# Strided sparse attention and a multiplicative FFN on one core: weight fold and first FFN tile laid between the attention phases of the first two batches

## The chip, the cores and the metric

The kernel runs on one NeuronCore of a Trainium2 chip. The metric is the device time of one execution in microseconds. Five engines take part: TensorE (PE in the profile; its weight loads are PEld) multiplies and transposes, VectorE (DVE), ScalarE (ACT) and GpSimd (POOL) copy, cast and do elementwise work, and SyncE (SP) issues the loads. Outputs are issued from ScalarE's queue.

## The reference

For 8 batches of 8 heads, with 576 positions and a head size of 64, masked attention is computed; heads 0 to 3 see the last 32 positions, heads 4 to 7 the earlier positions with the same remainder modulo 32. The heads are joined to 4608 tokens of 512 numbers, and a feed-forward stage follows that multiplies two projections.

```python
scores = scale * np.matmul(q, k.transpose(0, 1, 3, 2))
mask_local = (rel >= 0) & (rel < stride)                 # stride = 32
mask_strided = (rel >= 0) & (pos[None, :] % stride == pos[:, None] % stride)
attn = softmax(np.where(mask, scores, -1e9))
x = np.matmul(attn, v).transpose(0, 2, 1, 3).reshape(4608, 512)
out = ((x @ w1) * (x @ w2)) @ w3 @ w_out                  # w1, w2: 512x1024; w3: 1024x1024; w_out: 1024x512
```

## The kernel before

**The fold.** There is no nonlinearity between w3 and w_out, so the kernel multiplies them once into w34 (1024 x 512) and each token needs one product less. `fold_tr(jc)` (L353) transposes one block of 128 rows of w3 in eight transposes into one bank of PSUM, and copies the halves to w3T with VectorE and ScalarE. `fold_mm(jc)` (L362) is a sum of eight 512-wide matmuls, given in two halves of four, and one copy into w34. There are eight blocks.

**Attention.** A batch is four pairs of heads, two local and two strided. The work of a pair is a sequence of phases: `ph_T` (L208) transposes q and k; `ph_S` (L238) computes scores, exp on ScalarE and the mask on VectorE, in two groups; `ph_PV` (L259), once for each group, multiplies by v (with a column of ones for the sum) and divides on VectorE; `ph_T2` (L279) transposes the result into xT. `ph_R` (L225) transposes the last 64 positions of q and k, once for a batch. All phases of all batches form one list, `stream`; `batch_end[b]` is the place in it behind which xT holds batch b. Batch 0 has 21 phases, batch 1 has 25 (with the first transposes and scores of batch 2 among them), and each later one but the last has the same 25.

**The FFN.** A tile is 512 tokens, nine in all. `ab_halves` (L297) gives 16 units of four 512-wide matmuls: eight a and eight b, one of each for every 128 columns of w1 and w2; ScalarE copies a out of PSUM, VectorE multiplies it with b into abt. `o_halves` (L341) gives eight units of four matmuls with w34 for four output blocks, each copied by ScalarE and stored.

**Order.** The program order of all matmuls and transposes is kept (`pe`, L65). `host(units, upto, lead)` (L400) writes it: it emits the units one after the other, and after each beyond the first `lead` so many phases of the stream that it arrives at `upto` with the last unit. The order of instructions on the other engines is set when the kernel is built, with loads and casts early in the program. Buffers set further waits: psF has three banks for FFN sums (tag f), psB two for scores and attention products, psM one for transposes (tag m); loads land in nine staging buffers (stgp); cast w3 blocks have four buffers (w3n). A load is followed by a cast to fp16, by the engine named in the call: "p" GpSimd, "a" ScalarE, "v" VectorE.

**The opening.** Lines 411 to 427 give the loads: w3 block 0, w_out, w3 blocks 1 to 7, q, k and v of batch 0, w1 and w2 in four groups of 256 columns, then batch 1. Lines 429 to 446 place the fold first, with six phases of batch 0 laid between its last units, then the rest of batch 0 alone; then 12 units of FFN tile 0, four with a phase each, eight output units with a phase each, and the rest of batch 1 alone. From tile 1 on (L447), every tile's 24 units carry the 25 phases of the batch after next evenly.

Of the kernel before, what the change touches and what calls it, by code (L numbers as in the profile page):

```python
# [9 lines left out]
FP16 = mybir.dt.float16  # L10
# [9 lines left out]
def kernel(  # L20
# [11 lines left out]
    nc = tc.nc  # L32
# [4 lines left out]
    P = 128  # L37
# [3 lines left out]
    KF = DF // P  # L41
# [17 lines left out]
    psF = ctx.enter_context(tc.tile_pool(name="psF", bufs=3, space=bass.MemoryType.PSUM))  # L59
    psB = ctx.enter_context(tc.tile_pool(name="psB", bufs=2, space=bass.MemoryType.PSUM))  # L60
    psM = ctx.enter_context(tc.tile_pool(name="psM", bufs=1, space=bass.MemoryType.PSUM))
# [3 lines left out]
    def pe(ins):  # L65
        return tc.keep_in_program_order(ins)

    def copy(eng, out, in_):
        if eng == "a":
            nc.scalar.copy(out=out, in_=in_)  # L70
        elif eng == "v":
            nc.vector.tensor_copy(out=out, in_=in_)  # L72
        else:
            nc.gpsimd.tensor_copy(out=out, in_=in_)  # L74
# [47 lines left out]
    w1h = consts.tile([P, KM, DF], FP16)  # L122
    w2h = consts.tile([P, KM, DF], FP16)
    w34 = consts.tile([P, KF, DM], FP16)
# [8 lines left out]
    def load_wo(g, eng):  # L133
        src = moe_w_out.rearrange("(c p) n -> p c n", p=P)
        st = stgp.tile([P, 2, DM], FP32, tag="stg")
        nc.sync.dma_start(st, src[:, 2 * g:2 * g + 2, :])
        copy(eng, woh[:, 2 * g:2 * g + 2, :], st)

    def load_w3(jc, eng):
        st = stgp.tile([P, DF], FP32, tag="stg")  # L140
        nc.sync.dma_start(st, moe_w3[bass.ds(jc * P, P), :])
        t = ffn.tile([P, DF], FP16, tag="w3n", bufs=4)
        w3n[jc] = t
        copy(eng, t, st)

    def load_w12(g):
        cs = bass.ds(g * 256, 256)
        for wd, wh, eng in ((moe_w1, w1h, "p"), (moe_w2, w2h, "p")):
            st = stgp.tile([P, KM, 256], FP32, tag="stg")
            nc.sync.dma_start(st, wd.rearrange("(c p) n -> p c n", p=P)[:, :, cs])  # L150
            copy(eng, wh[:, :, cs], st)
# [4 lines left out]
    def load_qk(b, grp, engs="pp"):  # L156
        for nm, ten, eng in (("q", q, engs[0]), ("k", k, engs[1])):
            st = stgp.tile([P, 4, 4, D], FP32, tag="stg")
            nc.sync.dma_start(st.rearrange("p h c d -> p h (c d)"),
                              ten[b, 4 * grp:4 * grp + 4, 0:NM].rearrange("h (p c) d -> p h (c d)", c=4))  # L160
            t = qkp.tile([P, 4, 4, D], FP16, tag=f"{nm}{grp}")
            copy(eng, t, st.rearrange("p h c d -> p c h d"))
            x16[(b, nm, grp)] = t

    def load_rest(b, eng="p"):
        st = stgp.tile([P, H, D], FP32, tag="stg")
        for i, ten in enumerate((q, k)):
            nc.sync.dma_start(st[64 * i:64 * i + 64], ten[b, :, NM:S].rearrange("h p d -> p h d"))
        t = qkp.tile([P, H, D], FP16, tag="r")
        copy(eng, t, st)  # L170
        x16[(b, "r")] = t

    def load_vL(b):
        vt = v16L[b % 2]
        for hp in range(2):
            hs = slice(2 * hp, 2 * hp + 2)
            st = stgp.tile([P, 2, LT, D], FP32, tag="stg")
            for h in range(2):
                nc.sync.dma_start(st[32:P, h], v[b, 2 * hp + h].rearrange("(t p) d -> p t d", p=LQ))
            for pr in (bass.ds(32, 32), bass.ds(64, 64)):  # L180
                nc.gpsimd.tensor_copy(out=vt[pr, hs, :, 0:D], in_=st[pr])  # L181
            nc.vector.tensor_copy(out=vt[0:32, hs, 1:LT, 0:D], in_=vt[96:P, hs, 0:LT - 1, 0:D])

    def load_vS(b):
        vt = v16S[b % 2]
        for hp in range(2):
            st = stgp.tile([SQ, 2, ST, D], FP32, tag="stg")
            sf = st.rearrange("p h c d -> p h (c d)")
            sv = v[b, 4 + 2 * hp:6 + 2 * hp].rearrange("h (p c) d -> p h (c d)", c=ST)
            nc.sync.dma_start(sf[0:64], sv[0:64])  # L190
            nc.sync.dma_start(sf[64:SQ], sv[64:SQ])
            nc.gpsimd.tensor_copy(out=vt[:, 2 * hp:2 * hp + 2, :, 0:D], in_=st)
# [104 lines left out]
    def ab_halves(tch):  # L297
        tok = bass.ds(tch * NT, NT)
        res = []

        def first():
            abts[tch] = ffn.tile([P, KF, NT], FP16, tag="abt", bufs=4, name=f"abt{tch}")

        for jc in range(KF):
            st = {}

            def a(jc=jc, st=st):
                if jc == 0:
                    first()
                aps = psF.tile([P, NT], FP32, tag="f")  # L310
                for ci in range(KM):
                    pe(nc.tensor.matmul(aps, w1h[:, ci, bass.ds(jc * P, P)], xT[ci][:, tok],  # L312
                                        start=(ci == 0), stop=(ci == KM - 1)))
                asb = ffn.tile([P, NT], FP32, tag="asb")
                nc.scalar.copy(out=asb, in_=aps)  # L315
                st["asb"] = asb

            def bb(jc=jc, st=st):
                bps = psF.tile([P, NT], FP32, tag="f")
                for ci in range(KM):  # L320
                    pe(nc.tensor.matmul(bps, w2h[:, ci, bass.ds(jc * P, P)], xT[ci][:, tok],  # L321
                                        start=(ci == 0), stop=(ci == KM - 1)))
                nc.vector.tensor_mul(abts[tch][:, jc, :], bps, st["asb"])

            res += [a, bb]
        return res

    def acc_halves(lhs, rhs, done):
        st = {}

        def half(hf):
            if hf == 0:
                st["ps"] = psF.tile([P, NT], FP32, tag="f", name="ops")
            for ci in range(4 * hf, 4 * hf + 4):
                pe(nc.tensor.matmul(st["ps"], lhs(ci), rhs(ci), start=(ci == 0), stop=(ci == KF - 1)))  # L335
            if hf == 1:
                done(st["ps"])

        return [lambda: half(0), lambda: half(1)]

    def o_halves(tch):  # L341
        res = []
        for ts in range(NT // P):
            def done(ps, ts=ts):
                osb = ffn.tile([P, DM], FP32, tag="osb", bufs=3)
                nc.scalar.copy(out=osb, in_=ps)  # L346
                nc.scalar.dma_start(out_r[tch * (NT // P) + ts], osb)

            res += acc_halves(lambda ci, ts=ts: abts[tch][:, ci, bass.ds(ts * P, P)],
                              lambda ci: w34[:, ci, :], done)  # L350
        return res

    def fold_tr(jc):  # L353
        js = bass.ds(jc * P, P)
        ps = psM.tile([P, 1024], FP16, tag="m")
        for kc in range(KF):
            pe(nc.tensor.transpose(ps[:, kc * P:(kc + 1) * P], w3n[jc][:, bass.ds(kc * P, P)], id16))  # L357
        pv = ps.rearrange("x (c j) -> x c j", j=P)
        nc.vector.tensor_copy(out=w3T[0][:, :, js], in_=pv[:, 0:4, :])
        nc.scalar.copy(out=w3T[1][:, :, js], in_=pv[:, 4:8, :])  # L360

    def fold_mm(jc):  # L362
        js = bass.ds(jc * P, P)

        def done(ps):
            nc.vector.tensor_copy(out=w34[:, jc, :], in_=ps)

        return acc_halves(lambda kc: w3T[kc // 4][:, kc % 4, js], lambda kc: woh[:, kc, :], done)

# [2 lines left out]
    batch_end = {}  # L372
# [4 lines left out]
    for b in range(B):  # L377
# [4 lines left out]
        for i in range(4):  # L382
            p = 4 * b + i
# [14 lines left out]
    pos = [0]  # L398

    def host(units, upto, lead=0):  # L400
        n = len(units) - lead
        p0 = pos[0]
        for i, u in enumerate(units):
            u()
            tgt = p0 + ((upto - p0) * max(i + 1 - lead, 0)) // n
            while pos[0] < tgt:
                stream[pos[0]]()
                pos[0] += 1
# [2 lines left out]
    load_w3(0, "p")  # L411
    for g in range(4):
        load_wo(g, "p")
    for jc in range(1, KF):
        load_w3(jc, "p")
    load_qk(0, 0, "ap")
    load_rest(0, "p")
    load_vL(0)
    load_qk(0, 1, "ap")
    load_vS(0)  # L420
    for g in range(4):
        load_w12(g)
    load_qk(1, 0)
    load_rest(1)
    load_vL(1)
    load_qk(1, 1)
    load_vS(1)

    fold = []
    fold_tr(0)  # L430
    for jc in range(KF):
# [2 lines left out]
        if jc + 1 < KF:  # L434
            fold.append(lambda jc=jc: fold_tr(jc + 1))
        fold.append(h1)
    host(fold, 6, lead=17)
    host([lambda: None], batch_end[0])
    load_qk(2, 0)
    load_rest(2)  # L440
    load_vL(2)
    host(ab_halves(0), pos[0] + 4, lead=12)
    load_qk(2, 1)
    load_vS(2)
    host(o_halves(0), pos[0] + 8)
    host([lambda: None], batch_end[1])
    for tch in range(1, NTILE):  # L447
        units = ab_halves(tch) + o_halves(tch)
        if tch + 1 < B:
# [44 lines left out]
```

The softmax here doesn't subtract the row's maximum and nothing guards it: scores larger than these inputs give would overflow.

## Time and profile before

The median of three runs is 306.0 us (305.58 to 307.15); the profiled execution spans 304.4 us.

| engine | busy us | share of the span |
|---|---|---|
| TensorE | 275.4 | 90% |
| TensorE weight load | 146.7 | 48% |
| VectorE | 171.1 | 56% |
| ScalarE | 143.8 | 47% |
| GpSimd | 104.7 | 34% |

The kernel reads 38.80 MB and writes 9.44 MB. TensorE's mean granted clock is 0.954. In the chain that ended last, the matmuls of the FFN (L312, L321, L335) have 61% of the span. A row of a timeline gives start, duration, engine, line, operation, output and input, and in brackets how long the engine was idle before it and what ended that. A row of a table of stretches gives the busy time of each engine in turn with the number of its instructions, then clock, DMA share and GB/s. The clock is a share of full speed, and busy times grow when it falls.

### The profile page before, as it was taken

Reading aid. Unit: us, or ns where it says so; the run is one execution under the profiler, and the core shown is the slowest. Engines: PE = TensorE matmul, PEld = TensorE weight load, DVE = VectorE, ACT = ScalarE, POOL = GpSimd, SP = SyncE. Lnnn points to the kernel's source line nnn. Section 1 sums busy time; section 2 is a strip of 40 time slices with the busy share of each in tenths; the row PEclk is TensorE's granted clock in tenths of the full one; section 3 lists DMA queues with packets and bytes.
Section 4 is the critical chain, followed back from the end, with each engine's and each line's share of the span. In section 5 each row is a group of like instructions: output and inputs, shape, how many; then the busy total and the mean of one; then the engine's idle time right before and its main releaser. Section 6 shows DMA issues by size and latency. Waiting matters only on the chain.

```text
span 304.4 us, 6140 instructions
## 1 busy us (share of the span) xinstructions
PE 275.4 (90%) x2401; PEld 146.7 (48%) x2401; DVE 171.1 (56%) x357; ACT 143.8 (47%) x263; POOL 104.7 (34%) x120
## 2 busy tenths in 40 slices
PE   2498667999779999999999999999999999999995
PEld 1154444445554545555555555555555555444442
DVE  2043665325586795686588668856764775240330
ACT  2025573366553556545554655465555544433332
POOL 5766675750256750365366445210000000000000
PEclk9999965999857999999999999999999999999999
DMA  7999999951899954994899698021012002002003
GB/s 253 413 336 207 286 348 240 246 128 41 217 256 208 269 118 133 264 221 106 268 256 237 172 250 212 2 103 37 1 38 106 0 2 103 35 2 103 34 2 138
DMA packets 58653, 48.64 MB, mean 160 GB/s; under 512 B 29184, under 2 KB 49664, under 8 KB 58624
## 3 DMA queue, kind: packets, MB, share of 16 engines
q1 hardware_dynamic: 53440, 38.81, 50.7%
q10 hardware_dynamic: 5184, 9.44, 8.4%
q8 instruction: 19, 0.31, 0.5%
q14 instruction: 10, 0.08, 0.1%
HBM read 38.80 MB, written 9.44 MB: 158 GB/s over the span
## 4 chain that ended last, share of the span: by engine, by line
PE 78%; DVE 8%; ACT 7%; DMA 3%; issue 3%; SPq 1%; POOL 0%; ACTq 0%; DVEq 0%
PE ops L335 22%; PE bps L321 20%; PE aps L312 19%; PE ps L214 5%; PE xps L268 5%; DMA st<-in_moe_w_dram 3%; PE sps L248 3%; PE ps L284 2%; ACT pte L253 2%; DVE xqs L276 2%; PE ps L357 1%; DVE ptm_105 L255 1%; ACT xT_124 L291 1%; ACT qT L70 1%; ACT osb L346 1%
## 5 line engine op out<-in xcount | busy, mean ns | idle before, releaser
L315 ACT COPY asb<-aps 128x512 f32<-128x512 f32 x72 | 42.2, 586 | 67.2 <-PE aps L312 64.3
L74 POOL CAST t<-st 128x1024 f16<-128x1024 f32 (+1 forms) x46 | 45.1, 982 | 52.0 <-DMA st<-in_k_dram 41.6
L253 ACT ACTIVATE pte<-sps 128x576 f16<-128x576 f32 (+1 forms) x64 | 38.3, 649 | 9.1 <-PE sps L248 9.1
L321 PEld LDWEIGHTS <-w2h 128*128 128x128 f16 x288 | 26.3, 99 | 31.1 <-issue 5.5
L276 DVE TENSOR_TENSOR xqs<-xps,rcp 96x384 f16<-96x384 f32 (+1 forms) x64 | 39.6, 619 | 2.0
L312 PEld LDWEIGHTS <-w1h 128*128 128x128 f16 x288 | 25.7, 99 | 23.7 <-issue 1.9
L70 ACT COPY qT<-ps 128x512 f16<-128x512 f16 (+1 forms) x48 | 22.8, 481 | 26.3 <-PE ps L214 23.5
L346 ACT COPY osb<-ops 128x512 f32<-128x512 f32 x36 | 21.1, 586 | 29.4 <-PE ops L335 27.9
L312 PE MATMUL aps<-xT_124,w1h 128*128 128x512 f16 x72 | 27.8, 386 | 1.6 <-ACT xT_124 L291 1.5
L312 PE MATMUL aps<-xT_121,w1h 128*128 128x512 f16 x72 | 28.1, 390 | 0.0
L312 PE MATMUL aps<-xT_122,w1h 128*128 128x512 f16 x72 | 28.0, 388 | 0.0
L321 PE MATMUL bps<-xT_121,w2h 128*128 128x512 f16 x72 | 27.9, 388 | 0.0
L312 PE MATMUL aps<-xT_123,w1h 128*128 128x512 f16 x72 | 27.8, 386 | 0.0
L321 PE MATMUL bps<-xT_122,w2h 128*128 128x512 f16 x72 | 27.8, 386 | 0.0
L321 PE MATMUL bps<-xT_123,w2h 128*128 128x512 f16 x72 | 27.7, 385 | 0.0
L321 PE MATMUL bps<-xT_124,w2h 128*128 128x512 f16 x72 | 27.5, 382 | 0.0
L72 DVE COPY kT<-ps 128x512 f16<-128x512 f16 (+1 forms) x36 | 18.7, 534 | 9.8 <-ACT qT L70 9.8
L214 PE MATMUL ps<-id_79,t 128*128 128x128 f16 x256 | 20.8, 227 | 2.1 <-ACT w3T_130 L360 1.4
L214 PEld LDWEIGHTS <-t 128*128 128x128 f16 x256 | 17.6, 102 | 9.2 <-issue 3.5
L181 POOL CAST v16L_99<-st 32x768 f16<-32x768 f32 (+1 forms) x16 | 13.7, 854 | 18.5 <-PE xps L268 12.1
L274 DVE RECIPROCAL rcp<-xps 96x6 f32<-96x6 f32 (+1 forms) x64 | 12.2, 191 | 13.8 <-PE xps L268 13.5
L284 PE MATMUL ps<-id_79,xqs 72*128 72x72 f16 (+1 forms) x224 | 15.0, 210 | 3.7 <-DVE kT L72 1.6
(115 smaller groups left out, 408.8 us busy)
## 6 DMA issues: line engine op xcount, KB each, us to landing
out_dram<-osb ACTq DMA_DIRECT2D x36, 256.0 KB, 2.0
st<-in_moe_w_dram SPq DMA_DIRECT2D x16, 512.0 KB, 8.6
st<-in_q_dram SPq DMA_DIRECT2D x16, 512.0 KB, 7.1
st<-in_k_dram SPq DMA_DIRECT2D x16, 512.0 KB, 5.2
st<-in_v_dram SPq DMA_DIRECT2D x32, 144.0 KB, 4.2
st<-in_v_dram SPq DMA_DIRECT2D x16, 256.0 KB, 7.1
st<-in_moe_w_out_dram SPq DMA_DIRECT2D x4, 512.0 KB, 7.2
st<-in_q_dram SPq DMA_DIRECT2D x8, 128.0 KB, 10.3
```

The costliest lines, as they stand in the source:

```text
L70: nc.scalar.copy(out=out, in_=in_)
L72: nc.vector.tensor_copy(out=out, in_=in_)
L74: nc.gpsimd.tensor_copy(out=out, in_=in_)
L214: pe(nc.tensor.transpose(ps[:, i, c * P:(c + 1) * P], src[:, c, h0:h0 + 2].rearrange("p h d -> p (h d)"), id16))
L253: nc.scalar.activation(out=pte[0:kr], in_=sps[0:kr, :, 0:288], func=AF.Exp, bias=0.0, scale=scale)
L276: nc.vector.tensor_mul(xqs[0:w, 0:m].rearrange("p i h d -> p h i d"), xv[:, :, :, 0:D], _ap(rcp, 0, [[rp, w], [4, 2], [1, m], [0, D]]))
L284: pe(nc.tensor.transpose(ps[:, t * w:(t + 1) * w], s.xqs[t // m][0:w, t % m].rearrange("p h d -> p (h d)"), id16[0:w, 0:w]))
L312: pe(nc.tensor.matmul(aps, w1h[:, ci, bass.ds(jc * P, P)], xT[ci][:, tok], start=(ci == 0), stop=(ci == KM - 1)))
L315: nc.scalar.copy(out=asb, in_=aps)
L321: pe(nc.tensor.matmul(bps, w2h[:, ci, bass.ds(jc * P, P)], xT[ci][:, tok], start=(ci == 0), stop=(ci == KM - 1)))
L335: pe(nc.tensor.matmul(st["ps"], lhs(ci), rhs(ci), start=(ci == 0), stop=(ci == KF - 1)))
L346: nc.scalar.copy(out=osb, in_=ps)
```

## The change

The fold's units are laid across all 21 phases of batch 0, with four units ahead. FFN tile 0 is laid across batch 1: six units ahead, ten with a phase each, and eight output units across the 15 phases left. The loads are interleaved in the order in which the new program needs them: batch 0 comes between the blocks of w3, and batch 1 between the groups of w1 and w2. The fold's transposes take a bank of psF instead of the one of psM. Casts of w1 go to ScalarE, and those of batch 0's q, which were there, to GpSimd. The copies of the fold's products alternate between VectorE and ScalarE. The purpose is to give TensorE work of other kinds while a phase of attention waits for exp, mask or division. From tile 1 on the text of the kernel is as before.

```diff
-        for wd, wh, eng in ((moe_w1, w1h, "p"), (moe_w2, w2h, "p")):
+        for wd, wh, eng in ((moe_w1, w1h, "a"), (moe_w2, w2h, "p")):
...
-        ps = psM.tile([P, 1024], FP16, tag="m")
+        ps = psF.tile([P, 1024], FP16, tag="f", name="trp")
...
-            nc.vector.tensor_copy(out=w34[:, jc, :], in_=ps)
+            copy("va"[jc % 2], w34[:, jc, :], ps)
...
-    for jc in range(1, KF):
-        load_w3(jc, "p")
-    load_qk(0, 0, "ap")
-    load_rest(0, "p")
+    load_qk(0, 0)
+    load_rest(0)
+    load_w3(1, "p")
+    load_w3(2, "p")
     load_vL(0)
-    load_qk(0, 1, "ap")
+    load_w3(3, "p")
+    load_qk(0, 1)
+    load_w3(4, "p")
+    load_w3(5, "p")
     load_vS(0)
-    for g in range(4):
-        load_w12(g)
+    load_w3(6, "p")
+    load_w3(7, "p")
+    load_w12(0)
+    load_w12(1)
     load_qk(1, 0)
     load_rest(1)
+    load_w12(2)
     load_vL(1)
+    load_w12(3)
     load_qk(1, 1)
     load_vS(1)
...
-    host(fold, 6, lead=17)
-    host([lambda: None], batch_end[0])
+    host(fold, batch_end[0], lead=4)
     load_qk(2, 0)
     load_rest(2)
     load_vL(2)
-    host(ab_halves(0), pos[0] + 4, lead=12)
+    host(ab_halves(0), pos[0] + 10, lead=6)
     load_qk(2, 1)
     load_vS(2)
-    host(o_halves(0), pos[0] + 8)
-    host([lambda: None], batch_end[1])
+    host(o_halves(0), batch_end[1])
```

## The prediction

> **What bounds the kernel now.** I first read the slices of the whole span, to see where TensorE is not full.
>
> ```profile
> PE   2498667999779999999999999999999999999995
> ...
> PEclk9999965999857999999999999999999999999999
> DMA  7999999951899954994899698021012002002003
> ```
>
> A slice is 7.6 us. From slice 13 (about 99 us) to the end TensorE is full at the full clock: there only less TensorE work would help, and the change removes none. Everything to win lies in the first 13 slices, where TensorE is partly idle, its clock drops twice, and the DMA row is full until about 64 us. So I cut those 95 us at the borders of the work, which the timeline gives: second fold block (13.2), first transposes of batch 0 (27.6), the clock's first fall (40.5, the fold having ended at 37.4), first matmul of FFN tile 0 (51.3), clock back (54.6), end of that tile's outputs (78.2), first matmul of FFN tile 1 (90.7).
>
> ```profile
> 0.00:13.20 13.20, 3.35 (x13) 1.29 (x13) 1.79 (x14) 1.87 (x2) 8.58 (x20) 1.00 0.85 321
> 13.20:27.60 14.40, 14.09 (x93) 7.77 (x94) 6.27 (x12) 4.46 (x7) 8.73 (x9) 1.00 1.06 282
> 27.60:40.50 12.90, 8.08 (x96) 4.86 (x96) 6.67 (x14) 8.07 (x17) 9.04 (x9) 1.00 1.06 305
> 40.50:51.30 10.80, 7.08 (x105) 5.52 (x106) 7.66 (x17) 4.82 (x9) 6.69 (x6) 0.51 1.16 309
> 51.30:54.60 3.30, 3.30 (x13) 1.24 (x12) 0.00 (x0) 1.23 (x2) 1.73 (x3) 0.54 0.82 148
> 54.60:78.20 23.60, 22.89 (x171) 11.44 (x170) 10.67 (x22) 12.52 (x25) 9.48 (x10) 1.00 0.56 147
> 78.20:90.70 12.50, 8.40 (x128) 6.91 (x126) 8.79 (x19) 7.61 (x15) 6.09 (x7) 0.64 0.94 235
> 90.70:95.30 4.60, 4.60 (x21) 1.84 (x19) 2.60 (x6) 1.23 (x2) 3.20 (x4) 0.50 1.20 257
> ```
>
> After the stretch: its length, then busy time of TensorE, weight load, VectorE, ScalarE, GpSimd; then the clock, DMA share, GB/s. TensorE busy up to 90.7 sums to 67.2 us, so 23.5 us are idle. The worst rows are those in which attention runs with nothing between its phases: 40.5 to 51.3 and 78.2 to 90.7. There the clock also falls to half, and the FFN tile behind each pays for it: at 51.3 and at 90.7 it starts at half clock, and its matmuls run 0.63 us against 0.38 us later.
>
> Why attention alone is slow, the rows at batch 1's end show; each step waits for another engine (columns: start, duration).
>
> ```profile
> 79.92 1.19 ACT L253 ACTIVATE pte<-sps 72x576 f16<-72x576 f32 x2
> ...
> 80.60 0.86 DVE L255 TENSOR_TENSOR ptm_105<-pte,maskS 72x576 f16<-72x576 f16 x1 [2.24 <-ACT pte L253]
> ...
> 81.52 0.57 PE L268 MATMUL xps<-v16S_102,ptm_105 72*128 72x65 f16 x8 [1.03 <-DVE ptm_105 L255]
> ```
>
> The last view is when weights arrive. GpSimd casts each as it lands:
>
> ```profile
> 12.14 1.04 POOL L74 CAST t<-st 128x1024 f16<-128x1024 f32 x1 [0.24 <-DMA st<-in_moe_w_dram]
> ...
> 36.04 1.35 POOL L74 CAST w1h<-st 128x1024 f16<-128x1024 f32 x1 [0.23 <-DMA st<-in_moe_w_dram]
> ...
> 40.55 1.11 POOL L74 CAST w2h<-st 128x1024 f16<-128x1024 f32 x1 [0.46 <-DMA st<-in_moe_w_dram]
> ...
> 47.77 1.34 POOL L74 CAST w2h<-st 128x1024 f16<-128x1024 f32 x1 [1.59 <-DMA st<-in_moe_w_dram]
> ```
>
> w1/w2 are complete at 49.1, so even before, the FFN could not start much ahead of 51 with all its weights; but group 0 is there at 38.6 and group 1 at 41.7.
>
> **What the Trainium skill says.** "TensorE: Matmul & The Clock Gate", Part 1, has TensorE at half clock by default and after an idle window of about 3.4 us, and at full clock after about as long of sustained work. The trace agrees: half at 40.5 after six microseconds that were 58% busy, full again at 54.6, 3.3 us after dense work began. "PSUM — Partial Sum Buffer", Engine vs sequencer instructions, has the queues of ScalarE, VectorE and GpSimd strictly first-in first-out; no row here contradicts it, and it makes a cast on ScalarE a possible plug. "DMA: Bandwidth & Descriptors", Why small descriptors are slow, expects little from 256-byte pieces; the v loads of the local heads (L179, four issues in 6.56 us) agree: while they are issued at 21 to 27 us the rate falls from about 400 to between 89 and 216 GB/s.
>
> **The change part by part.**
>
> *Fold across batch 0.* No work is added: 8 folds of eight 512-wide matmuls at 0.216 us apart (13.8 us) and 64 transposes (8 in about 0.45, 3.6 us) stay. Before, they ran dense from 13.2 to 27.6 while attention waited for loads, then attention ran alone. Now q, k and the rest of batch 0 load ahead of w3 block 1. That block's cast stood at 12.14 behind 3.0 MB; 1.25 MB of batch 0 now go first, 3 us at about 400 GB/s or 4.5 with the small pieces. I take 16.5 for the restart of the fold (bounds 14 and 19). Remaining from there: about 16 us of fold (all but one transpose group and one half) and about 6 us of attention (a later tile of 27.8 us has 24 units of 0.86, which leaves 7.1 us for 25 phases, 0.28 each): 22 us, so 38.5 if TensorE never waits. The phases need latency: 21 phases beside 19 units, where the later tiles run 25 phases beside 24 units in 27.8 us, which shows that one unit per phase hides nearly all of it. The last w3 block comes last of the same 9.4 MB that before ended with the v cast at 34.77, so its transposes stand near 36.5, with three units and five phases left, 6 us (the last chain from scores to xT takes 4 to 5 of them at the rows above): 42.5, so the loads and not TensorE set it. I add 2 us for the copies of the fold, now queued between attention's copies (bounds 0 and 7: seven blocks, up to 1 us each). Batch 0 ends at about 44.5, against 51.3.
>
> *Fold transposes in the FFN banks.* Free of cost if a bank is free: three banks for one open sum, one transpose, one next. The single attention bank no longer alternates with the fold; before, the fold waited there 0.9 us for kT, and T (L214) 1.4 us for w3T. Gain 1 to 3 us, contained in the 44.5.
>
> *Product copies alternating, and casts.* Four copies of 0.69 us leave VectorE for 0.59 on ScalarE; q casts (two of 1.05 us) leave ScalarE for GpSimd, four w1 casts of about 1.04 come to it. Net ScalarE +4.4 us over 60 us in which it is about half to three quarters busy: hidden by TensorE's units. GpSimd falls by 2 us and is paced by loads anyway. The danger is order, not size: behind a waiting w1 cast stand the exps, on which VectorE's mask and then TensorE wait. Before, the two q casts on ScalarE stood after their loads and waited for nothing. Bounds 0 and 8 us; I take 1.
>
> *Tile 0 across batch 1.* Before: 12 units, four phases with four units, eight with eight output units, 13 phases alone. Now: 6 units, ten phases with ten units, 15 phases with eight output units. Six units take 5.2 us. Ten times 0.86 plus 0.4 for a phase (0.28 as in the later tiles, and a little of its latency) is 12.6. For the 15 phases I use what eight with eight took (68.5 to 78.2, 9.7 us) and 13 alone (12.5): about 1.0 a phase, 14.5 us. Sum 32.3. Loads of batch 1 now precede w1/w2 groups 2 and 3; group 3 was cast by 49.1, and about 1.9 MB with the slow v issue (6.8 us) go before it, so I place its casts at 56 to 57. Unit 12, the first that needs it, is due at 44.5 + 5.2 + 6 x 1.26 = 57; R(1), group 2 and the v of batch 1 come as close. I take 1 us of waiting (bounds 0 and 4). Tile 1 then starts at 44.5 + 32.3 + 1, about **78**, against 90.7.
>
> *Clock.* If units fill TensorE, the second drop goes: the 4.6 us at half clock after 90.7 save 2.3. So 306.0 - 12.7 - 2.3 = **291.0 us**.
>
> The limit below: 16.5 plus the rest of TensorE's work to that point. 67.2 less some 8 us for the halved clock (half of 7.1 at 40.5, half of 3.3 at 51.3, half of about 6 after 81.5) and less 5 done by then is 54, hence 70.5, and 306 - 20.2 - 2.3 = 283.5.
>
> **Rivals.**
> - *Filled as reckoned*, 287 to 296: 291, chance 0.55. For it: the later tiles have the same mixture at 99% busy.
> - *Loads and latency take half back*: the DMA row is full to 64 us in any order, and R(1), the v of batch 1 and group 3 each arrive late by 2 to 3 us; or the clock stays at half in 16 to 45, since waiting for w3 blocks leaves gaps. 7 us of delay and the clock saving lost give 291 + 7 + 2 = 300; chance 0.25. Against it: half-clock units are denser, and density brings the clock back.
> - *Nearly ideal*: no stall beyond the sum of work, 284 to 286: 285, chance 0.10.
> - *Plugged ScalarE, slower*: the casts of w1 groups 2 and 3 stand ahead of batch 0's last exps, which then wait for group 3 at 56. Batch 0 ends near 60, tile 0 and batch 1 take 33 after it: 93, and 306 + 2.3 = 308; chance 0.10. For it: the four casts are written ahead of all attention. Against it: so were the two q casts, which ran at 23.07 and 35.14, between copies and exps.
>
> **How the numbers follow.** Forecast 291. Low 284 covers the ideal case; high 302 covers the load case and leaves most of the plugged one out. Of the load case a little lies within 0.5% of 306, and of the plugged case a little too. Faster 0.87, same 0.04, slower 0.09.
>
> **What would show it.** Right: tile 1's first matmul near 78; no slice after the third with a clock of 6 or less; w3T copies alternating with exps up to 42; batch 0's end near 44; from then the distance of two tiles' starts near 28 us as before. Wrong: ScalarE rows at L74 that wait for in_moe_w with exps behind them (plugged); TensorE rows waiting for w1h, w2h or v16L_100 (loads); transposes at L357 waiting for the fold's copies (banks); clock at half between 16 and 60 (gaps). The forecast fails upward if two of these fall together, and downward if the first load of w3 block 1 lands by 13.

## The result and the profile after

The changed kernel takes **296.98 us** (median of 4 runs, 295.90 to 297.23), against 305.96 us of the kernel before: a ratio of 0.9693, with a 95% interval of 0.9658 to 0.9729. The profiled executions span 295.2 and 304.4 us. The forecast was 291.0, with a range of 284 to 302: right in direction and within the range, 6 us too low. In what follows a time is the median of all executions of a kernel, a ratio leaves out single slow ones, and some traces are of executions 2 to 6 us longer than that median, so moments are compared within one trace.

First the slices of the whole span.

```profile
PE   2258798999789999999999999999999999999995
...
PEclk9999999999999999999999999999999999999999
DMA  7999999999979929996999580120012002003003
```

Both falls of the clock are gone in this row. The holes in slices 5 to 7 and in slice 12 are smaller (7, 9, 8 and 8 tenths, before 6, 6, 7 and 7), though the slices are now 7.4 us long instead of 7.6. In the second and third slice TensorE does less than before. The next table cuts at the same events as the one in the prediction: waiting for the second fold block (10.4 to 18.0), that block at half clock (to 22.3), the rest of the fold and batch 0 (to 49.5, the first matmul of FFN tile 0), tile 0 and batch 1 (to 82.8, the first matmul of tile 1).

```profile
0.00:10.40 10.40, 3.35 (x13) 1.29 (x13) 1.79 (x14) 1.87 (x2) 6.49 (x18) 1.00 0.82 283
10.40:18.00 7.60, 0.00 (x0) 0.00 (x0) 0.00 (x0) 0.00 (x0) 4.79 (x5) 1.00 1.15 293
18.00:22.30 4.30, 4.26 (x17) 2.05 (x18) 1.15 (x3) 0.59 (x1) 2.70 (x4) 1.00 1.24 234
22.30:49.50 27.20, 22.61 (x276) 13.96 (x275) 16.28 (x35) 18.27 (x35) 16.13 (x16) 1.00 1.11 308
49.50:82.80 33.30, 30.36 (x308) 16.63 (x309) 19.64 (x40) 22.22 (x43) 20.57 (x22) 1.00 1.00 240
```

TensorE busy is the first number after the comma. It is zero for 7.6 us, and then 83% for 27 us: the fold did not fill batch 0 as reckoned. Tile 0 and batch 1 are at 91%. As times of the work:

| | before | forecast | after |
|---|---|---|---|
| second fold block starts | 13.2 | 16.5 | 18.0 |
| batch 0 done, tile 0 starts | 51.4 | 44.5 | 49.5 |
| tile 0's start to tile 1's start | 39.3 | 33.3 | 33.3 |
| tile 1 starts | 90.7 | 78 | 82.8 |
| from there to the end | 213.7 | 211.4 | 212.4 |

So nearly all of the 9.2 us between the two spans was won ahead of tile 1 (7.9 us), and of that 6.0 us in tile 0 and batch 1; the fold stage, which was to give 6.8 us, gave 1.9. Why TensorE stands empty here, the timelines of GpSimd and TensorE show (start, duration, engine, line, operation).

```profile
12.11 1.04 POOL L74 CAST t<-st 128x1024 f16<-128x1024 f32 x1 [0.45 <-DMA st<-in_q_dram]
14.42 1.04 POOL L74 CAST t<-st 128x1024 f16<-128x1024 f32 x1 [1.27 <-DMA st<-in_k_dram]
...
16.95 1.04 POOL L74 CAST t<-st 128x1024 f16<-128x1024 f32 x1 [0.44 <-DMA st<-in_moe_w_dram]
```

```profile
18.04 1.03 PE L357 MATMUL trp<-id_79,t 128*128 128x128 f16 x8 [8.12 <-POOL t L74]
...
22.28 1.02 PE L357 MATMUL trp<-id_79,t 128*128 128x128 f16 x8
23.14 0.61 PE L214 MATMUL ps<-id_79,t 128*128 128x128 f16 x8
```

Batch 0's q and k are cast at 15.5. Their transposes (L214) could follow at once, but in TensorE's written order four units of the fold and a third transpose group stand ahead, and all but the first of these wait for w3 block 1, cast at 18.0. After 8.1 us of idle time the eight transposes at 18.04 take 1.03 us, as those at 22.28 do, against 0.61 at 23.14: half clock, though the clock column says 1.00. TensorE had not been at full clock yet: the eight transposes at 5.30 took 1.03 us as well, and those at 5.31 and 13.24 in the kernel before. The Trainium skill, "TensorE: Matmul & The Clock Gate", has half clock in Part 1 as the state by default, until about 3.4 us of sustained work. The state is as it says; it lasted longer here, for 5.1 us of work from 18.04 to 23.14. So attention starts at 23.1, and its 21 phases then take 26.4 us.

### The profile page after: what moved, and what is told of

The parts are those of the page before. It is cut to its first block, busy times and chain, and to the rows that moved or that the text cites. A ratio compares the mean times of both kernels' runs of the same rounds, so it can differ in the third digit from the quotient of the medians.

```text
span 295.2 us, 6136 instructions
## 1 busy us (share of the span) xinstructions
PE 266.9 (90%) x2401; PEld 141.0 (48%) x2401; DVE 168.7 (57%) x353; ACT 147.1 (50%) x269; POOL 101.9 (35%) x118
## 4 chain that ended last, share of the span: by engine, by line
PE 73%; ACT 8%; DVE 7%; DMA 6%; issue 2%; SPq 2%; POOL 0%; ACTq 0%; DVEq 0%
PE ops L335 21%; PE bps L321 20%; PE aps L312 19%; PE ps L214 4%; PE xps L268 4%; DMA st<-in_moe_w_dram 3%; PE sps L248 3%; DMA out_dram<-osb 3%; ACT pte L253 3%; DVE xqs L276 2%; PE ps L284 2%; ACT xT_124 L291 2%; SPq L168 1%; ACT osb L346 1%; ACT qT L70 1%
## 5 line engine op out<-in xcount | busy, mean ns | idle before, releaser
L74 POOL CAST t<-st 128x1024 f16<-128x1024 f32 (+1 forms) x48 | 47.2, 990 | 36.4 <-DMA st<-in_k_dram 21.6
L321 PEld LDWEIGHTS <-w2h 128*128 128x128 f16 x288 | 25.7, 97 | 30.2 <-issue 4.7
L312 PEld LDWEIGHTS <-w1h 128*128 128x128 f16 x288 | 25.0, 98 | 22.3 <-ACT w1h L70 0.2
L312 PE MATMUL aps<-xT_124,w1h 128*128 128x512 f16 x72 | 27.3, 379 | 2.4 <-ACT xT_124 L291 2.2
L312 PE MATMUL aps<-xT_121,w1h 128*128 128x512 f16 x72 | 27.4, 381 | 0.1
L321 PE MATMUL bps<-xT_121,w2h 128*128 128x512 f16 x72 | 27.4, 381 | 0.0
L321 PE MATMUL bps<-xT_124,w2h 128*128 128x512 f16 x72 | 27.3, 379 | 0.0
L321 PE MATMUL bps<-xT_123,w2h 128*128 128x512 f16 x72 | 27.3, 379 | 0.0
L312 PE MATMUL aps<-xT_123,w1h 128*128 128x512 f16 x72 | 27.2, 378 | 0.0
L321 PE MATMUL bps<-xT_122,w2h 128*128 128x512 f16 x72 | 27.2, 378 | 0.0
L312 PE MATMUL aps<-xT_122,w1h 128*128 128x512 f16 x72 | 27.2, 378 | 0.0
L214 PEld LDWEIGHTS <-t 128*128 128x128 f16 x256 | 16.6, 98 | 8.4 <-issue 2.1
L214 PE MATMUL ps<-id_79,t 128*128 128x128 f16 x256 | 19.5, 219 | 1.0 <-DVE rcp L274 1.0
L181 POOL CAST v16L_99<-st 32x768 f16<-32x768 f32 (+1 forms) x16 | 13.8, 865 | 10.5 <-DMA st<-in_v_dram 7.6
L181 POOL CAST v16L_100<-st 32x768 f16<-32x768 f32 (+1 forms) x16 | 13.3, 834 | 11.6 <-PE xps L268 4.9
```

What stands on the lines that cost most here:

```text
L214: pe(nc.tensor.transpose(ps[:, i, c * P:(c + 1) * P], src[:, c, h0:h0 + 2].rearrange("p h d -> p (h d)"), id16))
```

## The experiments

Each ratio is to the kernel before on the same chip; a smaller ratio is faster.

**Which part gives what.** FFN tile 0 placed as before in the changed kernel:

```diff
-    host(ab_halves(0), pos[0] + 10, lead=6)
+    host(ab_halves(0), pos[0] + 4, lead=12)
...
-    host(o_halves(0), batch_end[1])
+    host(o_halves(0), pos[0] + 8)
+    host([lambda: None], batch_end[1])
```

> The changed kernel with FFN tile 0 placed as before (12 units ahead, four phases with four units, eight with eight, the rest alone); loads and fold as changed. If the gain comes from tile 0 laid across batch 1, as the two traces say (33.3 us from tile 0's start to tile 1's start, against 39.4, and a clock fall saved), the time is 304 to 306. If the fold and the loads brought it, 298 to 300.

302.55 us, ratio 0.986 (0.983 to 0.989). The same lines the other way round, in the kernel before and with nothing else changed:

> The kernel before with FFN tile 0 laid across batch 1 as in the change, and nothing else; loads, fold, banks and casts as before. If tile 0's place gives nearly all of it, 297 to 299 us. If it needs batch 1's earlier loads and the other edits, 301 to 304.

300.47 us, 0.980 (0.975 to 0.985). Neither reading was fully right: tile 0's place gives about 2.0% by itself, all the rest 1.4% by itself, and together they give 3.1%, nearly their sum. The part of tile 0, which seems the larger (the two intervals just meet), needs none of the other edits.

The loads of before (w3 complete, then batch 0, w1 and w2, batch 1) under the new order on TensorE:

> The changed kernel with the loads in the order of before (and batch 0's q cast on ScalarE as before): all of w3 first, then batch 0, then all of w1 and w2, then batch 1. If the order of loads is needed for the gain of the fold stage: attention again starts at about 27 with little left to lay between, batch 0 ends near 51 to 52, 299 to 302. If only the order on TensorE counts: with all of w3 early the fold runs without waiting, 296 to 298.

300.33 us, 0.979 (0.974 to 0.984), the first reading. In its trace the first attention transposes wait 3.97 us for q at 22.5, and tile 0 starts at 53.2. With the loads in the old order the rest of the change gives nothing measurable: this kernel is no faster than the one with tile 0's new place alone.

**The small edits.** The fold's transposes back in the attention bank (`psM`, tag m, in L355):

> The changed kernel with the fold's transposes back in the one bank of the attention transposes. If sharing that bank would cost, with seven transpose groups between the phases and about 1.2 us for the two copies that free the bank, each by up to 1 us: 299 to 304 us. If the FFN banks are as tight, or the waits fall into others: 297.

301.55 us, 0.983 (0.977 to 0.988), against 0.969 (0.966 to 0.973) of the changed kernel: the bank is worth about 4 us, or about 6 against the second measurement of the changed kernel below. The prediction had 1 to 3 us. Its trace shows the wait of TensorE:

```profile
24.52 0.61 PE L214 MATMUL ps<-id,t 128*128 128x128 f16 x8 [1.13 <-ACT w3T L360]
...
34.36 0.61 PE L214 MATMUL ps<-id,t 128*128 128x128 f16 x8 [1.13 <-ACT w3T L360]
```

An attention transpose waits here for ScalarE's copy of a fold block out of the one bank.

The casts of w1 back on GpSimd (`"p"` for `"a"` in L148):

> The changed kernel with the casts of w1 back on GpSimd. Theory C, ScalarE's casts stand between the exps: two w1 casts of 1.05 us ran on it at 43.3 and 46.0, in batch 0's last chain; without them batch 0 ends 1 to 2 us earlier, 295 to 296 us. Rival: they fill waits, GpSimd gets more casts and these slow VectorE's masks; 297 us or up to 1 us more.

296.93 us, 0.967 (0.962 to 0.972): no difference from 0.969. Where ScalarE casts w1 in batch 0 it delays nothing that shows in the time: in the changed kernel the copy of xT at 46.9 stands behind the cast at 46.0, but the copy after it again waits 0.63 us for TensorE. All product copies on VectorE (L366):

> The changed kernel with all eight copies of the fold's products on VectorE. Four copies of 0.69 us return to VectorE and four of 0.59 leave ScalarE. If VectorE's queue holds up masks and divisions of batch 0, 298 to 299; if ScalarE's does, 295 to 296; if neither, 297.

295.64 us, 0.9615 (0.957 to 0.966), by the number the reading in which ScalarE's queue holds up batch 0. But the changed kernel, measured once more beside other kernels, gave this:

> The changed kernel itself, to compare the two others with on one chip: 296 to 298 us.

295.87 us, 0.9625 (0.957 to 0.968). So its ratio differs by 0.7% between two comparisons, and neither of the last two edits is told from it.

**Why the fold stage gave little.** Two w3 blocks ahead of q and k:

```diff
-    load_qk(0, 0)
-    load_rest(0)
     load_w3(1, "p")
     load_w3(2, "p")
+    load_qk(0, 0)
+    load_rest(0)
```

> The changed kernel with w3 blocks 1 and 2 loaded ahead of batch 0's q and k (297.0 us otherwise). Theory A, a starved start: TensorE stands empty from 10.4 to 18.0 us because w3 block 1 comes behind q, k and the rest, and that delay is carried to the end; then the second fold transposes come at about 13 instead of 18.0, batch 0 ends 4 us earlier and the time is 292 to 294. Theory B, latency of batch 0: what ends batch 0 is the chain of its phases through ScalarE and VectorE, begun by q and k; these now land 2.5 us later, and the time is 297 to 299.

295.67 us, 0.964 (0.959 to 0.970). The transposes came at 13.5, as theory A had it, but the time did not follow: it lies between the two readings, and is not told from the changed kernel. In its trace TensorE then waited 3.8 us at 26.4 for the next block, whose cast stands on GpSimd behind the four casts of v. Then the other side, attention in front:

```diff
-    host(fold, batch_end[0], lead=4)
+    fold[0]()
+    host([lambda: None], 4)
+    host(fold[1:], batch_end[0], lead=3)
```

> The changed kernel with batch 0's first four phases (both transposes of the first two pairs, the rest and the first scores) placed ahead of the second fold transposes, loads as changed. In the changed kernel q and k are cast at 15.5, but the first attention transposes come at 23.1, behind fold units that wait for w3 block 1 until 18.0. Theory B2, TensorE's written order makes attention wait and batch 0's 21 phases then need 26 us: batch 0 ends 3 to 6 us earlier, 291 to 294 us. Theory A, the w3 blocks' lateness itself sets the end: no change, 297.

297.43 us, 0.965 (0.960 to 0.971). Its timeline of TensorE:

```profile
13.09 0.61 PE L214 MATMUL ps<-id,t 128*128 128x128 f16 x4 [3.22 <-POOL t L74]
...
44.97 1.27 PE L312 MATMUL aps<-xT,w1h 128*128 128x512 f16 x4
...
63.33 0.40 PE L214 MATMUL ps<-id,t 128*128 128x128 f16 x4 [2.06 <-POOL t L74]
66.33 0.61 PE L214 MATMUL ps<-id,t 128*128 128x128 f16 x4 [2.60 <-POOL t L74]
```

The written order, not the arrival of w3, kept batch 0 late. With attention in front tile 0 starts at 45.0, half a microsecond from the forecast 44.5, although the last w3 block was cast later in this trace than in the changed kernel's (38.8 against 37.0). So batch 0's end moved as theory B2 had it, and yet the time is the one that theory A named. In this trace the four to five microseconds were given back at 63: the transposes of batch 1's third pair wait for q and then k of its strided heads, and GpSimd cast that k at 65.2. How much of this wait belongs to this one trace is not known. But the limit stands in both traces of the changed kernel too, the first and the second measurement:

```profile
62.01 1.22 POOL L74 CAST t<-st 128x1024 f16<-128x1024 f32 x1 [1.67 <-DMA st<-in_k_dram]
...
64.19 0.61 PE L214 MATMUL ps<-id_79,t 128*128 128x128 f16 x8
```

```profile
63.76 1.04 POOL L74 CAST t<-st 128x1024 f16<-128x1024 f32 x1 [2.73 <-DMA st<-in_k_dram]
...
64.85 0.40 PE L214 MATMUL ps<-id,t 128*128 128x128 f16 x4 [0.45 <-POOL t L74]
```

In the first k is ready at 63.2 and its transposes follow at 64.2 without a wait; in the second k is ready at 64.8, and they wait 0.45 us for it. As long as k arrives so, an earlier fold stage can bring them forward by about 1 us at most: its lateness was hidden by this load.

**Is it that load?** The four loads of v for batch 1's local heads left out (v is zero there, set at the start), with attention in front:

> The kernel with batch 0's first phases in front, and v of batch 1's local heads not loaded but zero (four loads of 144 KB and two casts less, so its output is not the reference's). Theory D, loads of batch 1 take the gain back: with the fold stage repaired, batch 0 ended at 45.0, as forecast, but the third transposes of batch 1 then waited until 66 for k; without the slow v loads that k comes some 5 us earlier, tile 0 to tile 1 shrinks from 41 to 33 to 36 us, and the time is 290 to 293. If instead the phases of batch 1 themselves are slow, 295 to 297.

296.53 us, 0.964 (0.960 to 0.969): theory D missed, and the time is that of the other reading. The k cast came at 60.0, 5 us earlier as expected, and TensorE did not wait for it. But the third pair's transposes stood at 63.5 all the same. TensorE now waited 1.3 and 0.9 us for ScalarE's copies of kT, and ran at half clock around 57. On ScalarE these rows lie between the copies:

```profile
52.20 1.05 ACT L70 CAST w1h<-st 128x1024 f16<-128x1024 f32 x1
...
55.17 1.07 ACT L70 CAST w1h<-st 128x1024 f16<-128x1024 f32 x1
56.12 0.29 ACT L70 COPY kT<-ps 128x128 f16<-128x128 f16 x1
```

So I tried the reverse: loads complete, but w1 cast on GpSimd, product copies on VectorE, and eight units of tile 0 ahead (`lead=8`).

> Batch 0's first four phases in front, the fold's copies on VectorE, the casts of w1 on GpSimd, and eight units of tile 0 ahead instead of six; loads as in the changed kernel. With the fold stage repaired batch 0 ends at 45. If what then took the gain back was ScalarE, whose w1 casts stand before the copies of batch 1's transposes, and the wait for k of its strided heads, both are gone or covered and tile 1 starts at 78 to 80: 291 to 294, below the changed kernel's 296 to 297. If batch 1's chain of 25 phases at 1.05 to 1.1 us each sets it, whatever is repaired before, tile 1 stays at 81 to 83: 295 to 297.

297.72 us, 0.971 (0.966 to 0.976), nearest to the second reading and a little above it. Tile 0 starts at 46.9, ScalarE is free, and the third pair waits for k again:

```profile
65.56 0.40 PE L214 MATMUL ps<-id,t 128*128 128x128 f16 x4 [1.46 <-POOL t L74]
...
83.14 0.81 PE L312 MATMUL aps<-xT,w1h 128*128 128x512 f16 x3
```

Last, loads in order of need: v, q and k of batch 1 ahead of the last groups of weights.

```diff
-    load_w12(2)
     load_vL(1)
-    load_w12(3)
+    load_w12(2)
     load_qk(1, 1)
+    load_w12(3)
...
-    host(ab_halves(0), pos[0] + 10, lead=6)
+    ab0 = ab_halves(0)
+    host(ab0[:12], pos[0] + 11, lead=8)
+    host(ab0[12:], pos[0] + 4)
```

with attention in front and product copies on VectorE.

> Batch 0's first four phases in front; the fold's copies on VectorE; q and k of batch 1's strided heads and its v loaded ahead of the last groups of w1 and w2; tile 0 with eight units ahead, four units over eleven phases, four over four, eight over the last ten. If loads of batch 1 in the order of need are what is missing, its chain starts earlier and the last group of weights is waited for by filler only: 291 to 294. If the sum of bytes until then is the limit whatever the order, 295 to 297.

298.23 us, 0.972 (0.968 to 0.976), slower than both readings. Here the rival "plugged ScalarE" is seen at work, first on ScalarE and then on TensorE:

```profile
60.72 1.04 ACT L70 CAST w1h<-st 128x1024 f16<-128x1024 f32 x1 [2.30 <-DMA st<-in_moe_w_dram]
61.67 0.58 ACT L70 COPY qT<-ps 128x512 f16<-128x512 f16 x1
62.15 0.59 ACT L70 COPY kT<-ps 128x512 f16<-128x512 f16 x1
62.63 1.20 ACT L253 ACTIVATE pte<-sps 128x576 f16<-128x576 f32 x2
```

```profile
63.84 0.51 PE L268 MATMUL xps<-v16L,ptm 128*128 128x65 f16 x6 [4.40 <-ACT pte L253]
```

The last w1 cast waits for its load, copies and exps stand behind it, and TensorE waits 4.4 us.

**What sets the end.** From the transposes of batch 1's third pair (where q and k came apart, those of k), tile 1 follows 17.6 to 20.5 us later in these traces:

| kernel | tile 0 starts | third pair of batch 1 | tile 1 starts | last step |
|---|---|---|---|---|
| changed | 49.5 | 64.2 | 82.8 | 18.6 |
| changed, second measurement | 49.4 | 64.9 | 83.1 | 18.2 |
| product copies on VectorE | 48.1 | 62.7 | 81.4 | 18.7 |
| w3 blocks 1 and 2 first | 48.4 | 67.1 | 87.6 | 20.5 |
| attention in front | 45.0 | 66.3 | 86.2 | 19.9 |
| and v of batch 1 not loaded | 45.2 | 63.5 | 82.7 | 19.2 |
| and no w1 cast on ScalarE | 46.9 | 65.6 | 83.1 | 17.6 |
| one bank for fold and attention | 53.0 | 68.3 | 86.7 | 18.3 |
| only tile 0's place changed | 52.1 | 68.2 | 86.2 | 18.0 |

The last step is 19 phases with 10 or 11 units, about 1 us a phase. Where tile 0 starts at 52 or 53, the third pair follows from it; where it starts at 45 to 47, and with w3 blocks first, the rows of the traces put it down to the load or to ScalarE. In no trace does tile 1 start ahead of 81. No kernel tried is told apart from the changed one as faster.

## Why the prediction was right, and where it was off

- **The place of the gain** was right: 7.9 of the 9.2 us were won before tile 1, and the other 1.3 us from there to the end, for the clock saved. I had 2.3 there; the first a of tile 1 now waits 0.72 us for xT, whose copy stands behind two exps of batch 2 on ScalarE.
- **Tile 0 across batch 1** was right in size, 33.3 us forecast and measured. Its parts came at 5.4, 13.2 and 14.7 us against 5.2, 12.6 and 14.5. That it fits to a tenth is partly luck: by the prediction's own figures (22.2 us for 21 phases) the last part comes to 15.9, not 14.5, and the 1 us added for waiting was meant for loads, for which TensorE waited only 0.2 us here.
- **The mis-sized term is "Batch 0 ends at about 44.5"**, 5.0 us too early. The step that failed is "so the loads and not TensorE set it". The last w3 block was cast at 37.0, near the forecast, and from its transposes to the end it took 6.1 us, as reckoned; but these transposes stood at 43.5, 6.4 us behind their data, because of what was written ahead of them. Attention could not start before 23.1, behind units that waited for w3, and its 21 phases took 26.4 us, 1.26 each. In the later tiles, on which I rested that one unit per phase hides nearly all of a phase's latency, a phase takes 1.11 (27.8 us for 25). The restart was at 18.0 and not 16.5, and the half clock after it (18.0 to 23.1, some 2.5 us lost) was not reckoned; but with attention in front the fold restarts at 20.2, at half clock too, and the same stage ends at 45.0. Of the signs of being wrong only the half clock came to any size; the written order was not among them.
- **The clock** of the kernel before was read too simply. I had its falls agree with the skill's idle window of about 3.4 us. Before those at 40.5 and 81.5 TensorE was 58% busy for 6 us and 47% for 3.5 us, with no gap longer than 1.1 us: an idle window is not what these rows show, and what brings the falls about stays open.
- **The loads rival** gave 300 and said that loads of batch 1 take half back. In part that is what happens even with that stage repaired: with v loaded, k of the strided heads is cast between 61 and 66, where 78 us for tile 1 needed it at 59 (an estimate: 78 less the 18.6 of the table). I had considered R(1), v and the last weights, and not this k. Between 291 and 300 the measured 297 lies nearer to this rival than to my forecast.
- **Plugged ScalarE** did not happen in this kernel (297 with the casts on either engine), and does in the last experiment, in which the order of the loads and the places of attention and tile 0 differ.
- **The bank** was worth 4 to 6 us in the new order, not 1 to 3; the forecast held it within the 44.5.
- Open: the version with neither the load, nor ScalarE's casts, nor the fold's order in the way was not run, so it is not shown that tile 1 could start at 78.

## What to carry to other kernels

Filler helps where something can be computed beside the latency; it hurts where the filler itself waits for a load and stands ahead of work whose data are there, since TensorE's program order is kept: here it stood idle until 18.0 with q and k cast at 15.5. Before sizing a repair of one stage, look up when the next stage's last input arrives: a stage can be 5 us late and lose nothing by it, when a later load is no earlier. An edit in two independent places is best measured place by place; here the forecast had 6.8 us for the fold stage and 6.0 for tile 0 with batch 1, and they gave 1.9 and 6.0.

## What the runs showed of the hardware

VectorE's mask (L255, two fp16 inputs from SBUF) took 0.44 to 0.46 us in all 32 cases of the kernel before in which no GpSimd cast ran beside it, and up to 1.33 us in the 32 others. In the changed kernel's batch 0, from the timelines of VectorE and GpSimd:

```profile
28.95 0.46 DVE L255 TENSOR_TENSOR ptm_105<-pte,maskL 128x576 f16<-128x576 f16 x1 [0.79 <-ACT pte L253]
29.98 1.31 DVE L255 TENSOR_TENSOR ptm_106<-pte,maskL 128x576 f16<-128x576 f16 x1
```

```profile
29.95 1.04 POOL L74 CAST t<-st 128x1024 f16<-128x1024 f32 x1 [1.27 <-PE xps L268]
```

The Trainium skill, "SBUF — State Buffer", says in the section on the two separate sides that an instruction of VectorE with two SBUF inputs and one of GpSimd that reads SBUF take a shared pair of ports in turn, each for its whole length. The trace agrees with that: the second mask begins with the cast at 29.98 and ends 0.3 us after it, at 31.29, where the first, with no cast beside it, takes 0.46. No experiment took the casts away, so the lock is the skill's account and not shown here. Three masks of batch 0 were slowed so, at 30.0, 36.2 and 46.6, by 0.6 to 0.9 us each; for the first two TensorE then waited 0.66 and 0.85 us. That casts for later stages lengthen the phases of this one was in no step of the prediction.
